# 1/sigma of a layer norm on all 128 partitions at once, in place of a column form that is spread by transposes

## The chip, the cores and the metric

The kernel runs on one core of one Trainium2 chip. The metric is the device time of one launch in microseconds (us). TensorE (PE) multiplies matrices; its weight loads are listed apart, as PEld. VectorE (DVE), ScalarE (ACT) and GpSimd (POOL) work on elements; SyncE (SP), POOL and ACT issue DMAs. An "execution" below is one profiled launch.

## What is computed

Four batches of 768 rows and 512 features go through a chunked attention, a mixer block and a second block. The change lies in the mixer block:

```python
u = x + mixed                                    # mixed: real part of a 2D FFT of x
mu = np.mean(u, axis=-1, keepdims=True)
var = np.mean((u - mu) ** 2, axis=-1, keepdims=True)
un = (u - mu) / np.sqrt(var + 1e-06)
ch = np.maximum(un @ w_ch1, 0.0) @ w_ch2
return (u + ch)
```

Since 1/sigma is one positive number for each row, the kernel multiplies the centred `u - mu` by both weight matrices first and scales the result by 1/sigma at the end.

## The kernel before, in words

Features lie on the partitions and rows of the batch in the free dimension. A *chunk* is 384 rows of one batch (`TC`), so there are eight; its centred input is `us`, four tiles of 128 features. Every matrix product is made of three float32r products of high and low parts (`split3`), accumulated in PSUM; line 65 issues nearly all of them.

Three stages follow each other. First the attention, the Fourier products and a first quarter of the mixer's hidden units (f = 0 to 3), in an order written out by hand (`SCHED`). Then the mixer's other hidden units, f = 4 to 15, in a loop over *steps* `s` and hidden tiles `f`; this is where the change is. Last the second block (`b1`, `conv`, `gate`, `b2`).

In the middle stage each turn of the loop runs `g1(s, f)` (12 products into a PSUM tile `h`; ACT takes the high part `hh`, DVE the low part `hl`), then a piece of the statistics, then `g2` of an earlier f (12 products into four `acc` tiles; two turns late, or one at the ends of a step). Chunks 0 to 4 are done in two steps (five hidden tiles, then seven); chunks 5 to 7 in one step of twelve. So the statistics generator `prep_stat(s)` runs eight times, one part for each turn `j` of the step: squares on ACT at j = 0, two adds on DVE at j = 1, nothing at j = 2, the sum over features at j = 3 (`pvar`), 1/sigma at j = 4, and at j = 5 the spreading (`prow`). `finish(s)` adds the `acc` tiles to `yp` and multiplies by the spread row `rb` (`d["r"]`).

Between these parts DVE and ACT decode weights for the next stage (`late()`, tiles `wsc`, `wlb`, `whb`, `wo`), paced by `PACE`, and split the next step's input into `uh` and `ul` (`split_uc`, at the last turn but one). Each engine executes its instructions in program order. The PSUM pool of `h`, `pvar` and `prow` has three buffers.

In the last chunk the loop also loads the second block's first input: `x_load(0, hf)` for the two halves, through the tile tag `sq` of the statistics, which has one buffer; each generator has three parts (the DMA on SP's queue, then twice a high part on ACT and a low part on DVE).

Where tiles lie (bytes from the start of a partition, as the program places them): pool `a1p` (`uh`, `ul`, `hh`, `hl`, `rb`) begins at 31,968 and is followed by `uc1` (`us`, `yp`, `sq` of 6,144 bytes each, and `st`, which takes 128) at 71,904; `wrb`, with the weight tiles of f = 8 to 15, at 90,464; `wra`, with the weight tiles of f = 4 to 7, at 163,808, where the last stage has its weights `wit`; `rx` at 196,576. In the last stage `xh` and `xl` of even batches lie in `rx`, those of odd batches in pool `w3p`, from byte 98,720 on. Weight slices are multiples of 512 bytes apart, slices of `uh`, `hh` and `xh` multiples of 1,536.

Of the kernel before, what the change touches and what calls it, by code (L numbers as in the profile page):

```python
# [7 lines left out]
F32 = mybir.dt.float32  # L8
F32R = mybir.dt.float32r
AF = mybir.ActivationFunctionType  # L10
ALU = mybir.AluOpType
# [14 lines left out]
TC = 384  # L26
# [19 lines left out]
def fourier_mixer_kernel(ctx: ExitStack, tc: tile.TileContext, qk, vw, w1, w2, w_in, w_out, conv_w,  # L46
                         mask, ident, dtab, orow, stab, sgn, out):
    nc = tc.nc
    mm = nc.tensor.matmul
# [12 lines left out]
    def accumulate(o, seq, start=True, stop=True):  # L62
        n = len(seq)
        for i, (a, b) in enumerate(seq):
            mm(o, a, b, start=(start and i == 0), stop=(stop and i == n - 1))  # L65

    const = ctx.enter_context(tc.tile_pool(name="const", bufs=1))
    epsc = const.tile([128, 1], F32, name="epsc")
    nc.vector.memset(epsc, 1e-6)
    onesm = const.tile([128, 128], F32, name="onesm")  # L70
# [5 lines left out]
    ident_sb = const.tile([128, 128], F32, name="ident_sb")  # L76
    stg = ctx.enter_context(tc.tile_pool(name="stg", bufs=2))
    rx = ctx.enter_context(tc.tile_pool(name="rx", bufs=1, side="right"))
    a1p = tc.alloc_tile_pool(name="a1p", bufs=2)
    ps_g = tc.alloc_tile_pool(name="ps_g", bufs=PSG, space=PSUM)  # L80
# [86 lines left out]
    def run(gen, n=1):  # L167
        for _ in range(n):
            if next(gen, "end") == "end":
                return False  # L170
        return True

    def rxt(tag, name):
        return rx.tile([128, 512 * NI], F32R, tag=tag, name=name)[:, 0:4 * TC].rearrange("p (k t) -> p k t", k=4)
# [3 lines left out]
    for nm, dst in (("a", w1h), ("b", w1l), ("c", w2h), ("d", w2l)):  # L178
        t = rx.tile([128, 512 * NI], F32R, tag=f"rx{nm}", name=f"rx{nm}")
# [329 lines left out]
    def x_load(b, hf, pool, tag="us"):  # L509
        ss = slice(hf * TC, hf * TC + TC)  # L510
        t = pool.tile([128, 4, TC], F32, tag=tag, name="xs")
        nc.sync.dma_start(out=t, in_=ucd[b][:, :, ss])
        yield
        if b % 2:
            xh, xl = (w3p.tile([128, 4, TC], F32R, tag=f"{n}{hf}", name=n) for n in ("xh", "xl"))
        else:
            xh, xl = rxt(("rxb", "rxa")[hf], "xh"), rxt(("rxd", "rxc")[hf], "xl")
        for k in range(0, 4, 2):
            if k:
                yield  # L520
            nc.scalar.copy(xh[:, k:k + 2], t[:, k:k + 2])
            nc.vector.tensor_tensor(out=xl[:, k:k + 2], in0=t[:, k:k + 2], in1=xh[:, k:k + 2].bitcast(F32),
                                    op=ALU.subtract)
        xs[b, hf] = (xh, xl)
# [53 lines left out]
    with tc.manual_schedule():  # L578
# [43 lines left out]
        ps_g.release()  # L622
        ps_g = tc.alloc_tile_pool(name="ps_g2", bufs=3, space=PSUM, reuse_waits="tile")
        uc1 = tc.alloc_tile_pool(name="uc1", bufs=1, reuse_waits="tile")
        NC1 = NB * S // TC
        NTC = TC // 128

        FS = (range(NI, NI + NGA), range(NI + NGA, NF1), range(NI, NF1))
        steps = [(c, FS[p], p == 1) for p in range(2) for c in range(NG2)] + [(c, FS[2], True) for c in range(NG2, NC1)]
        ck = {}  # L630

        def half(c):
            b, hf = divmod(c, 2)
            return b, slice(hf * TC, hf * TC + TC)

        def prep_load(s):
            b, ss = half(steps[s][0])
            us = (uc1.tile([128, 4, TC], F32, tag="us", name="us") if s % 3 == 0
                  else rxt(("rxa", "rxc")[s % 3 - 1], "us").bitcast(F32))
            nc.sync.dma_start(out=us, in_=ucd[b][:, :, ss])  # L640
            ck[s] = {"us": us}
# [7 lines left out]
        def late():  # L649
            stage = rx.tile([128, 512 * NI], F32, tag="rxd", name="wo")  # L650

            def place2(f):
                o = f[1] % 2 * 1024
                return stage[:, o:o + 512], stage[:, o + 512:o + 1024]

            yield from decode_all([(w_in[f], place2, ("i", f), wihd[f]) for f in range(NF2)]
                                  + [(w_out[f], place2, ("o", f), wohd[f]) for f in range(NF2)])
# [7 lines left out]
        def prep_stat(s):  # L665

            d = ck[s]
            c = steps[s][0]
            b, ss = half(c)
            sq = uc1.tile([128, 4, TC], F32, tag="sq", name="sq")  # L670
            for j in (0, 2):
                nc.scalar.activation(out=sq[:, j:j + 2], in_=d["us"][:, j:j + 2], func=AF.Square)
            nc.gpsimd.dma_start(out=ucd[b][:, :, ss], accum_op=ALU.add,
                                in_=mud[b][:, ss].rearrange("o (k t) -> o k t", k=1).to_broadcast([128, 4, TC]))
            yield
            nc.vector.tensor_tensor(out=sq[:, 0:2], in0=sq[:, 0:2], in1=sq[:, 2:4], op=ALU.add)
            nc.vector.tensor_tensor(out=sq[:, 0], in0=sq[:, 0], in1=sq[:, 1], op=ALU.add)
            yield
            yield
            p = ps_g.tile([128, 512], F32, tag="g", name="pvar")  # L680
            for t in range(NTC):
                mm(p[:, t:t + 1], sq[:, 0, t * 128:t * 128 + 128], onesm[:, 0:1], start=True, stop=True)
            st = uc1.tile([128, 4, NTC], F32, tag="st", name="st", bufs=2)
            ve, sd, r, e = (st[:, i] for i in range(4))
            nc.vector.tensor_scalar(out=ve, in0=p[:, 0:NTC], scalar1=0.5, scalar2=1e-6, op0=ALU.mult, op1=ALU.add)
            nc.scalar.activation(out=sd, in_=p[:, 0:NTC], func=AF.Sqrt, bias=epsc[:, 0:1], scale=0.5)
            yield
            nc.vector.reciprocal(out=r, in_=sd)
            nc.vector.tensor_tensor(out=e, in0=r, in1=r, op=ALU.mult)
            nc.vector.tensor_tensor(out=e, in0=e, in1=ve, op=ALU.mult)  # L690
            nc.vector.tensor_scalar(out=e, in0=e, scalar1=-0.5, scalar2=1.5, op0=ALU.mult, op1=ALU.add)
            nc.vector.tensor_tensor(out=r, in0=r, in1=e, op=ALU.mult)
            yield
            p = ps_g.tile([128, 512], F32, tag="g", name="prow")
            for t in range(NTC):
                nc.tensor.transpose(p[:, t * 128:t * 128 + 128], r[:, t:t + 1].to_broadcast([128, 128]), ident_sb)
            d["r"] = a1p.tile([128, TC], F32, tag="y", name="rb")
            nc.scalar.copy(d["r"], p[:, 0:TC])

        def g2(s, f):  # L700
            d = ck[s]
# [39 lines left out]
        stat, xg = iter(()), []  # L741
        for i, (s, f) in enumerate(seq):
            c, fs, last = steps[s]
            j, K = f - fs[0], len(fs)
            pace += [r for a, r in PACE if i >= a][-1]
            while pace >= 1.0:
                pace -= 1.0
                if not run(todo["W"]) and dec is None:
                    dec = todo["W"] = late()
            g1(c, f)  # L750
            if j == JL and s + 1 < len(steps):
                prep_load(s + 1)
            if j == 0 and last:
                stat = prep_stat(s)
            run(stat)
            if j == 2:
                prep_y(s)
            if j == K - JS and s + 1 < len(steps):
                for _ in split_uc(steps[s + 1][0], ck[s + 1]["us"]):
                    pass  # L760
            if s + 1 == len(steps):
                if j == 4:
                    for _ in todo["W"]:
                        pass
                    xg = [x_load(0, hf, uc1, "sq") for hf in range(2)]
                if 4 <= j < 10:
                    run(xg[(j - 4) // 3])
                if j == 7:
                    for n in range(NF2):
                        kind, fw = order[n]  # L770
                        wit.append(wra.tile([128, 1024], F32R, tag=f"w{kind}_{fw}", name=f"wit{n}"))
                        nc.gpsimd.dma_start(out=wit[n], in_=wihd[n])
            upto = i - 1 if i in ends or i - 1 in ends else i - 2
            while done <= upto:
                g2(*seq[done])
                done += 1
# [84 lines left out]
    with tc.manual_schedule():  # L861
        for h in hrow:
# [8 lines left out]
                                       op0=ALU.bitwise_and, op1=ALU.bitwise_or)  # L871
        nc.vector.tensor_scalar(out=cwi[1], in0=cwd[:, :, 1], scalar1=0xFFFFF, scalar2=0x100000,
                                op0=ALU.bitwise_and, op1=ALU.bitwise_or)
# [4 lines left out]
                                       op0=ALU.mult, op1=ALU.mult)  # L878
# [4 lines left out]
        for i in range(len(steps) + LAG):  # L883
# [12 lines left out]
            if i < len(steps):  # L896
                conv(b, f)
                if f == 0 and b + 1 < NB:
                    xg = [x_load(b + 1, hf, xsp) for hf in range(2)]
# [123 lines left out]
```

## Time and profile before

| what | value |
| --- | --- |
| median of 3 runs | 1041.53 us (1041.39 to 1042.96) |
| the profiled execution's own time | 1035.2 us |
| its span, first to last instruction | 1033.4 us |
| PE busy | 1019.8 us, 99% of the span |
| DVE, ACT, POOL busy | 638.1, 448.6, 187.7 us |
| granted TensorE clock | 0.998 of full speed |

The span is what the views of the trace divide; the profiled execution took 1.8 us more than its span, and 6.3 us less than the median of the runs. A matmul's listed duration overlaps the next one's, so the pace of a row of products is read from the distance of their starts, or from the chain of waits, which gives each piece of the path its own length.

### The profile page before, as it was taken

How to read it: one execution, taken by the hardware profiler on the slowest of the kernel's cores; microseconds unless marked ns; L12 is line 12 of the kernel's file. 1: busy time of each engine (PE TensorE's matmuls, PEld its weight loads, DVE VectorE, ACT ScalarE, POOL GpSimd, SP SyncE). 2: the span in 40 equal slices, each digit the busy share in tenths (PEclk: the TensorE clock that was granted, in tenths of full speed). 3: DMA queues.
4: the chain of work that ended last, by engine and by line, in shares of the span. 5: the costliest groups of instructions: out<-in, count | busy, mean ns of one | idle time of the engine just before them, and what ended most of it. 6: DMA issues, size and time to landing. Idle time of an engine off the chain costs nothing.

```text
span 1033.4 us, 16896 instructions
## 1 busy us (share of the span) xinstructions
PE 1019.8 (99%) x6548; PEld 972.6 (94%) x6548; DVE 638.1 (62%) x1489; ACT 448.6 (43%) x939; POOL 187.7 (18%) x215
## 2 busy tenths in 40 slices
PE   9999999999999999999999999999999999999998
PEld 7988989999999999999999999999989999999997
DVE  6788956757788765765565553513348656565554
ACT  6875665654434433333223232312236454454442
POOL 1442341422300000100000000001013222222222
PEclk9999999999999999999999999999999999999999
DMA  7854432521336555586989775353553211010101
GB/s 264 263 163 127 137 115 58 177 72 70 127 99 228 179 164 189 178 170 147 192 176 225 153 204 110 91 103 90 165 134 113 72 62 62 1 62 1 62 1 61
DMA packets 63776, 130.87 MB, mean 127 GB/s; under 512 B 4887, under 2 KB 39167, under 8 KB 63471
## 3 DMA queue, kind: packets, MB, share of 16 engines
q1 hardware_dynamic: 51424, 102.35, 29.9%
q0 software_dynamic: 12016, 27.16, 14.7%
q8 instruction: 51, 0.84, 0.3%
q10 hardware_dynamic: 256, 0.28, 0.1%
q14 instruction: 29, 0.24, 0.1%
HBM read 92.28 MB, written 43.79 MB: 132 GB/s over the span
## 4 chain that ended last, share of the span: by engine, by line
PE 92%; DVE 4%; DMA 2%; ACT 1%; issue 1%; POOL 0%; DVEq 0%; POOLq 0%; ACTq 0%
PE acc L65 32%; PE h L65 25%; PE ph L65 12%; PE y L65 7%; PE o L266 3%; PE z L65 3%; PE p L65 3%; PE sc L232 3%; PE atp L255 2%; PE idle L206 1%; DVE sm L238 1%; PE xtp L291 1%; DMA wot<-wohd 1%; DVE ul L165 1%; PE pm L415 1%
## 5 line engine op out<-in xcount | busy, mean ns | idle before, releaser
L65 PE MATMUL acc<-hh,w 128*128 128x384 f32 x768 | 211.2, 338 | 0.0
L65 PE MATMUL h<-uh,w 128*128 128x384 f32 x768 | 209.8, 337 | 0.0
L486 DVE SCALAR_TENSOR_TENSOR hl<-h,hh 128x384 fp32r<-128x384 f32 x128 | 70.5, 555 | 201.5 <-ACT hh L485 201.2
L485 ACT ACTIVATE hh<-h 128x384 fp32r<-128x384 f32 x128 | 62.4, 490 | 278.9 <-PE h L65 278.8
L65 PEld LDWEIGHTS acc<-hh,w 128*128 128x128 f32 x768 | 140.5, 188 | 0.0
L65 PEld LDWEIGHTS h<-uh,w 128*128 128x128 f32 x768 | 140.4, 188 | 0.0
L65 PE MATMUL ph<-xh,wit 128*128 128x384 f32 x512 | 136.3, 337 | 2.2 <-ACT hrow L813 2.2
L65 PE MATMUL acc<-hl,w 128*128 128x384 f32 x384 | 129.4, 337 | 0.1
L65 PE MATMUL h<-ul,w 128*128 128x384 f32 x384 | 129.2, 337 | 0.0
L65 PE MATMUL acc<-wot,hgh 128*128 128x512 f32 x384 | 119.7, 393 | 0.0
L821 DVE SCALAR_TENSOR_TENSOR cv<-hrow,cw_sb,cv 128x768 f32<-128x768 f32 x64 | 111.8, 1747 | 3.1 <-ACT cv L815 2.0
L65 PEld LDWEIGHTS ph<-xh,wit 128*128 128x128 f32 x512 | 93.3, 188 | 4.0 <-ACT hrow L813 2.8
L833 POOL TENSOR_TENSOR hgl<-cv,hgh 128x768 fp32r<-128x768 f32 x32 | 59.8, 1868 | 196.6 <-ACT hgh L832 174.5
L827 DVE TENSOR_TENSOR cv<-hrow,cv 128x768 f32<-128x768 f32 x32 | 30.7, 959 | 98.9 <-ACT cv L826 98.9
L65 PE MATMUL ph<-xl,wit 128*128 128x384 f32 x256 | 86.1, 336 | 0.0
L65 PEld LDWEIGHTS acc<-wot,hgh 128*128 128x128 f32 x384 | 71.7, 188 | 13.4
L246 ACT ACTIVATE sm<-sm,ngm 96x128 f32<-96x128 f32 x256 | 80.2, 393 | 5.8 <-DVE ngm L238 5.8
L813 ACT ACTIVATE hrow<-ph 128x384 f32<-128x384 f32 x64 | 31.2, 493 | 102.3 <-PE ph L65 101.1
L65 PE MATMUL acc<-wot,hgl 128*128 128x512 f32 x192 | 74.7, 389 | 0.0
L65 PEld LDWEIGHTS acc<-hl,w 128*128 128x128 f32 x384 | 72.2, 188 | 0.4 <-DVE hl L486 0.4
L65 PEld LDWEIGHTS h<-ul,w 128*128 128x128 f32 x384 | 72.1, 188 | 0.0
L238 DVE CUSTOM_DVE_ANT_0 sm<-sc,mask_sb 96x128 f32<-96x128 f32 x256 | 56.4, 282 | 15.7 <-PE sc L232 13.9
(145 smaller groups left out, 1836.8 us busy)
## 6 DMA issues: line engine op xcount, KB each, us to landing
w<-in_w SPq DMA_DIRECT2D x32, 512.0 KB, 3.9
qk<-in_qk SPq DMA_DIRECT2D x32, 448.0 KB, 4.0
us<-ucd SPq DMA_DIRECT2D x13, 768.0 KB, 5.3
yp<-yd SPq DMA_DIRECT2D x13, 768.0 KB, 9.1
vw<-in_vw SPq DMA_DIRECT2D x32, 260.0 KB, 3.1
ucd<-uc SPq DMA_DIRECT2D x8, 768.0 KB, 4.3
yd<-y SPq DMA_DIRECT2D x32, 192.0 KB, 2.4
ucd<-mud POOLq DMA_DIRECT2D x8, 768.0 KB, 17.3
```

The lines of the kernel that those rows point to most:

```text
L65: mm(o, a, b, start=(start and i == 0), stop=(stop and i == n - 1))
L232: mm(sch[2 * a + g], qT[64 * g:64 * g + 64, a, :], kT[64 * g:64 * g + 64, a, :], start=True, stop=True)
L238: nc.vector.tensor_tensor_reduce(out=sm[:, h, :], in0=sch[h], in1=mask_sb[:, kind, :], op0=ALU.add, op1=ALU.min, scale=-0.125, scalar=3e38 ...
L246: nc.scalar.activation(out=d["ex"][:, h, :], in_=d["ex"][:, h, :], func=AF.Exp, scale=-1.0, bias=d["ngm"][:, h:h + 1])
L255: nc.tensor.transpose(at[:, i, :], d["ex"][:, 4 * half + i, :], ident_sb[:QB, :QB])
L266: mm(oh[:, h // 4, h % 4, :], at_sb[:, h, :], vw[:, h * (HD + 1):(h + 1) * (HD + 1)], start=True, stop=True)
L485: nc.scalar.activation(out=hh, in_=p[:, 0:TC], func=AF.Relu)
L486: nc.vector.scalar_tensor_tensor(out=hl, in0=p[:, 0:TC], scalar=0.0, in1=hh.bitcast(F32), op0=ALU.max, op1=ALU.subtract)
L813: nc.scalar.activation(out=h[:, 1 + hf * TC:1 + hf * TC + TC], in_=p[:, 0:TC], func=AF.Relu)
L821: nc.vector.scalar_tensor_tensor(out=cv, in0=h[:, j:j + S], scalar=cw_sb[:, j, f:f + 1], in1=cv, op0=ALU.mult, op1=ALU.add)
L827: nc.vector.tensor_tensor(out=cv, in0=h[:, 1:S + 1], in1=cv, op=ALU.mult)
L833: nc.gpsimd.tensor_tensor(out=hgl[i], in0=cv, in1=hgh[i].bitcast(F32), op=ALU.subtract)
```

## The change

The sum over features becomes two float32r products with the 128 x 128 matrix of equal weights as stationary operand. Their result has the variance of all 384 rows on every partition, so 1/sigma is computed there on 128 x 384 elements in place of 128 x 3, and nothing is spread afterwards. The squares are split into a float32r part and a rest for it. The intermediate values reuse planes of `sq`; so the loads that go through `sq` in the last chunk move from j = 4 to j = 6.

```diff
         uc1 = tc.alloc_tile_pool(name="uc1", bufs=1, reuse_waits="tile")
+        onesr = uc1.tile([128, 128], F32R, name="onesr")
+        nc.vector.tensor_copy(onesr, onesm)
         NC1 = NB * S // TC
-        NTC = TC // 128
...
             nc.vector.tensor_tensor(out=sq[:, 0], in0=sq[:, 0], in1=sq[:, 1], op=ALU.add)
+            sqr = uc1.tile([128, 2, TC], F32R, tag="sqr", name="sqr")
+            nc.scalar.copy(sqr[:, 0], sq[:, 0])
+            nc.vector.tensor_tensor(out=sqr[:, 1], in0=sq[:, 0], in1=sqr[:, 0].bitcast(F32), op=ALU.subtract)
             yield
             yield
             p = ps_g.tile([128, 512], F32, tag="g", name="pvar")
-            for t in range(NTC):
-                mm(p[:, t:t + 1], sq[:, 0, t * 128:t * 128 + 128], onesm[:, 0:1], start=True, stop=True)
-            st = uc1.tile([128, 4, NTC], F32, tag="st", name="st", bufs=2)
-            ve, sd, r, e = (st[:, i] for i in range(4))
-            nc.vector.tensor_scalar(out=ve, in0=p[:, 0:NTC], scalar1=0.5, scalar2=1e-6, op0=ALU.mult, op1=ALU.add)
-            nc.scalar.activation(out=sd, in_=p[:, 0:NTC], func=AF.Sqrt, bias=epsc[:, 0:1], scale=0.5)
-            yield
-            nc.vector.reciprocal(out=r, in_=sd)
+            accumulate(p[:, 0:TC], [(onesr, sqr[:, i]) for i in range(2)])
+            ve, e = sq[:, 2], sq[:, 3]
+            r = d["r"] = a1p.tile([128, TC], F32, tag="y", name="rb")
+            nc.vector.tensor_scalar(out=ve, in0=p[:, 0:TC], scalar1=0.5, scalar2=1e-6, op0=ALU.mult, op1=ALU.add)
+            nc.scalar.activation(out=sq[:, 1], in_=p[:, 0:TC], func=AF.Sqrt, bias=epsc[:, 0:1], scale=0.5)
+            yield
+            nc.vector.reciprocal(out=r, in_=sq[:, 1])
+            yield
             nc.vector.tensor_tensor(out=e, in0=r, in1=r, op=ALU.mult)
             nc.vector.tensor_tensor(out=e, in0=e, in1=ve, op=ALU.mult)
             nc.vector.tensor_scalar(out=e, in0=e, scalar1=-0.5, scalar2=1.5, op0=ALU.mult, op1=ALU.add)
             nc.vector.tensor_tensor(out=r, in0=r, in1=e, op=ALU.mult)
-            yield
-            p = ps_g.tile([128, 512], F32, tag="g", name="prow")
-            for t in range(NTC):
-                nc.tensor.transpose(p[:, t * 128:t * 128 + 128], r[:, t:t + 1].to_broadcast([128, 128]), ident_sb)
-            d["r"] = a1p.tile([128, TC], F32, tag="y", name="rb")
-            nc.scalar.copy(d["r"], p[:, 0:TC])
...
+                if j == 6:
                     xg = [x_load(0, hf, uc1, "sq") for hf in range(2)]
-                if 4 <= j < 10:
-                    run(xg[(j - 4) // 3])
+                if 6 <= j < 12:
+                    run(xg[(j - 6) // 3])
```

In `uc1` the change adds `onesr` (512 bytes) and `sqr` (3,072) and drops `st`; `wrb`, which follows, then begins at byte 93,920 in place of 90,464. `a1p`, `wra`, `rx` and `w3p` stay where they are.

## Rows read from the trace of the kernel before

**Rows 1.** The page, part 1: busy time, share of the span, instructions.

```profile
PE 1019.8 (99%) x6548; PEld 972.6 (94%) x6548; DVE 638.1 (62%) x1489; ACT 448.6 (43%) x939; POOL 187.7 (18%) x215
```

**Rows 2.** Busy time by stretch: the middle stage with the statistics.

```profile
440.00:758.00 318.00, 318.00 (x1839) 317.68 (x1838) 152.97 (x302) 87.87 (x159) 22.05 (x23) 1.00 0.64 148
```

**Rows 3.** Chain of waits, 440 to 770 us: start, length, what; first and last statistics.

```profile
463.07 0.56 PE pvar L682 x6
463.63 2.22 PE acc L65 x12
...
472.18 0.33 PE prow L696 x3
472.51 2.11 PE acc L65 x12
...
480.96 2.11 PE h L65 x12
...
718.70 0.56 PE pvar L682 x6
...
727.76 0.33 PE prow L696 x3
```

**Rows 4.** Chain of waits, 345 to 445 us: f = 4 to 8.

```profile
379.44 2.08 PE acc L65 x12
381.53 2.11 PE h L65 x12
...
387.80 2.08 PE h L65 x12
389.88 2.11 PE acc L65 x12
```

**Rows 5.** Chain of waits, last stage: an even batch, then an odd one.

```profile
808.18 4.19 PE ph L65 x24
...
816.49 4.24 PE ph L65 x24
```

**Rows 6.** Groups by line and form: shapes, count, busy us, mean ns.

```profile
L677 DVE TENSOR_TENSOR sq<-sq 128x384 f32<-128x384 f32 x8 | 4.5, 558 | 0.3
L294 DVE TENSOR_SCALAR xT<-xtp 128x384 f32<-128x384 f32 x1 | 0.5, 544 | 0.0
L123 DVE TENSOR_SCALAR wsc<-w 128x512 int32<-128x512 int32 x48 | 21.7, 452 | 3.0 <-DMA w<-in_w 1.4
L688 DVE RECIPROCAL st<-st 128x3 f32<-128x3 f32 x8 | 1.3, 167 | 0.0
L269 DVE RECIPROCAL r<-r 96x8 f32<-96x8 f32 x32 | 6.4, 199 | 1.1
L698 ACT COPY rb<-prow 128x384 f32<-128x384 f32 x8 | 3.8, 474 | 0.0
```

**Rows 7.** Chain of waits, 160 to 180 us: a plain float32 product of 384 columns.

```profile
166.92 0.67 PE pm L415 x2
```

**Rows 8.** Timeline of DVE, turns 1 and 4 to 6 of the first statistics.

```profile
458.81 0.56 DVE L677 TENSOR_TENSOR sq<-sq 128x384 f32<-128x384 f32 x1
...
468.59 0.56 DVE L486 SCALAR_TENSOR_TENSOR hl<-h,hh 128x384 fp32r<-128x384 f32 x1 [2.41 <-ACT hh L485]
...
473.90 1.83 DVE L165 TENSOR_TENSOR ul<-us,uh 128x768 fp32r<-128x768 f32 x2 [0.54 <-ACT uh L162]
...
477.35 0.56 DVE L486 SCALAR_TENSOR_TENSOR hl<-h,hh 128x384 fp32r<-128x384 f32 x1 [1.02 <-ACT hh L485]
```

**Rows 9.** Timeline of the last chunk: SP's load, DVE's turn 5, ACT's last turn.

```profile
719.35 15.81 SPq L512 DMA_DIRECT2D xs<-ucd  x2
...
728.38 0.56 DVE L486 SCALAR_TENSOR_TENSOR hl<-h,hh 128x384 fp32r<-128x384 f32 x1 [2.75 <-ACT hh L485]
...
753.47 0.49 ACT L485 ACTIVATE hh<-h 128x384 fp32r<-128x384 f32 x1 [3.73 <-PE h L65]
```

**Rows 10.** Instructions by tile, `xs`: time from issue to landing.

```profile
DMA to landing us min/median/max: 6.7/7.9/9.1
```

## Prediction

> **What bounds the kernel now.** I read the page's busy times first, then the chain of waits through the stage that holds the change, then the busy times of that stretch, then single groups and timelines for prices. The page shows PE busy for 99% of the span, the next engine for 62% [rows 1]. In the stretch from 440 to 758 us PE is busy all 318.00 us and DVE 152.97 of them, 48% [rows 2]. The chain of waits runs through PE alone there: products in groups of 12, and for each of the eight chunks one piece of `pvar` and one of `prow` between them [rows 3]. So in this stage an instruction costs what it lengthens PE's row, and work on DVE or ACT costs nothing until PE waits for it. The first group behind `pvar` is listed with 2.22 us where others have 2.11 [rows 3]; those 0.11 us belong to `pvar`.
>
> The same view has a second thing to see. Groups of 12 products do not all take the same time: 2.08 us with the weights of f = 4 to 7, 2.11 with those of f = 8, both for `h` and for `acc`, side by side in one step [rows 4]. In the last stage 24 `ph` products take 4.19 us in an even batch and 4.24 in an odd one [rows 5]. The work is the same; what differs is the pool in which an operand lies: weights in `wra` against `wrb`, `xh` in `rx` against `w3p`. The places of front explain it in one way: all fast operands begin 224 bytes past a multiple of 256 (31,968, 163,808, 196,576), the weights in `wrb` 96 bytes past one (90,464), `xh` in `w3p` 160 (98,720). They allow another: slow operands lie in the middle of the partition, between 90,464 and 163,808, fast ones outside.
>
> **The change part by part.** *PE, removed.* `pvar` costs 0.56 + 0.11 = 0.67 us, `prow` 0.33 [rows 3]: 1.00 us for a chunk, 8.0 for eight.
>
> *PE, added.* Two products of 128x128 by 128x384 float32r, the form of `h` and `acc`: 2.11 / 12 = 0.176 us each [rows 3], 0.35 for a chunk, 2.8 for eight. Net gain 8.0 - 2.8 = 5.2 us. A bound from the other side is the plain float32 product of 384 columns, 0.67 us [rows 7]: two of these, 1.34, would cost 8 x 0.34 = 2.7 us more than what goes. I take the float32r price, since both operands are declared so.
>
> *Placement.* `wrb` moves from 90,464 to 93,920, which is 224 past a multiple of 256, like every fast operand. It holds the weights of eight of the twelve hidden tiles: 5 x 24 products in the first steps, 5 x 7 x 24 in the second, 3 x 8 x 24 in the long ones, 1,536 in all or 128 groups of 12. If they fall to the fast pace, 128 x (2.11 - 2.08) [rows 4] = 3.8 us are gained on top; if place in the partition is what counts, nothing, as `wrb` stays in the middle. I take the 3.8, because the second reading needs the range of slow places to end within some 11,700 bytes between the last weights of `wrb` (151,904) and the first of `wra`, while the first covers rows of two stages, weights and moving data, with one rule. Both ends stay in the range.
>
> [...]
>
> *DVE.* Gone for a chunk are seven tiny operations less the one that stays, about 6 x 0.16 = 1.0 us with the reciprocal's 0.167 [rows 6]. New at 384 columns: four TENSOR_TENSOR of 0.558 (one subtract, three in the correction), a TENSOR_SCALAR from PSUM of 0.544, one from SBUF of about 0.452 x 384 / 512 = 0.34 [rows 6], and the reciprocal. The trace has this only at 3 columns (0.167) and 8 (0.199), 6.4 ns for a column [rows 6]: 0.167 + 381 x 0.0064 = 2.6 us. Below, it is bounded by the 0.558 of a TENSOR_TENSOR; I take 2.6, as the slope comes from the operation itself. Together 2.23 + 0.54 + 0.34 + 2.6 - 1.0 = 4.7 us for a chunk, 38 for eight: DVE's 153 of 318 us become 191, 60%. ACT gets a copy, a longer root, and loses the copy of `rb`: under 0.5 us a chunk.
>
> What hides it, in the times of the first chunk [rows 8, 3]: `hl` of turn 4 ends at 469.15, the reciprocal at 471.8, a piece of decoding (0.7) at 472.5, and `hl` of turn 5 comes at 472.8 as before. Behind it the four correction operations (2.0), `ul` of the next step (1.83) and a piece of decoding end at 478.0, and `hl` of turn 6 moves from 477.35 to 478.0. PE needs `ul` at 480.96 and that `hl` after it. With ACT's decoding copies that queue behind DVE's, I count 3 us of cover. So the price is zero up to a reciprocal of some 5.6 us.
>
> *The wait added.* PE now waits for the subtract at turn 1. The second add ends at 459.4 [rows 8], ACT's copy (0.47) and the subtract (0.56) at 460.5; PE comes to `pvar` at 463.07 [rows 3]. Behind it on PE stand all products, but there are 2.6 us to spare. `h` tiles fare better: `prow` no longer takes one of three PSUM buffers.
>
> *The moved loads.* Before, SP started the first load at 719.35, once `pvar` had read `sq` [rows 9]. Now it must wait until the correction has read `sq` at turn 5, 728.9 + 2.0 = 731, and lands by 738.9 at the median, 740.1 at worst [rows 10]; conversions follow at turns 7 and 8. The second load starts near 743 and lands by 752.1 at worst; its conversions at turns 10 and 11 queue behind the last `hh` at 753.47 [rows 9], whose 24 last products give 4 us more. SP has nothing urgent behind these loads. Price zero; were a landing 4 us later, about 3 us once.
>
> *Onesr.* One DVE copy, under 0.2 us, once, beside PE's work.
>
> **Sum.** 5.2 + 3.8 = 9.0 us less on PE's row. The profiled execution would go from 1035.2 to 1026.2, its span from 1033.4 to 1024.4; the runs, whose median lies 6.3 us above the profiled execution, from 1041.5 to 1032.5.
>
> **The rivals.** *A, the forecast*: both gains, 1032.5. *B, the products in `wrb` keep 2.11*: only the 5.2 us, 1036.3. [...] *C, `wrb` at some third pace*, since 224 past a multiple of 256 is seen for weights only at 480 past a multiple of 512, and 93,920 is 224 past: anything from 1030 to 1041. *D, slower: the reciprocal.* If it takes over 5.6 us, `ul` of the next step is late and PE stands at the first `h` of each following step; from 6.7 us (17 ns a column, 2.7 times the slope of the rows) it eats the whole gain, at 8 us it costs 8 x 2.4 = 19 us, 1051.7. *E, no gain: the sum runs as plain float32* and the pace in `wrb` stays: 1041.5 + 2.7 = 1044.2.
>
> **How the numbers follow.** Chances: A 0.50, B 0.33, C 0.08, D 0.05, E 0.04. The likeliest is 1032.5. The range reaches from a little under A to a little over B, since the two hold most of the chance: 1030.5 to 1037.5; the one or two us beyond them are for the scatter of the runs (1041.39 to 1042.96). Faster by over 0.2% (2.1 us, about what a measurement of this kernel can tell from no change): A, B and most of C and a little of D, 0.92; within it: 0.04; slower: 0.04.
>
> **What would show it.** In the profile after: PE still at 99%; in the chain two products of `pvar` in about 0.35 us a chunk, no `prow`; groups of f = 8 and above at 2.08 (A) or 2.11 (B); RECIPROCAL 128x384 near 2.6 us; no wait of PE for `ul`, `hl` or `pvar`'s operands; the first `ph` as soon after the last `acc` as before. The forecast is wrong if the chain in this stage leaves PE, or if those groups stay at 2.11.

## The result, and the profile after

The median of four runs goes from 1041.47 us (1041.39 to 1042.96) to 1031.78 us (1027.97 to 1032.75); the ratio is 0.9903, with a 95% interval of 0.9885 to 0.9921. The forecast was 1032.5, with a range of 1030.5 to 1037.5.

The page's first part after the change, to be read beside [rows 1]:

```profile
PE 1015.4 (99%) x6492; PEld 968.1 (94%) x6492; DVE 674.1 (65%) x1498; ACT 452.8 (44%) x939; POOL 187.9 (18%) x215
```

PE still fills the span. DVE grew by 674.1 - 638.1 = 36.0 us, and PE did not wait for it but for one gap of 0.2 us. Busy time in the middle stage, up to the end of its last product (columns as in [rows 2]):

```profile
440.00:753.70 313.70, 313.70 (x1810) 313.46 (x1809) 192.23 (x318) 93.46 (x163) 23.45 (x25) 1.00 0.68 158
```

DVE is at 192.23 of 313.70 us, 61%, where it had 48%. The chain of waits, 440 to 770 us, which answers to [rows 3] (start, length, what):

```profile
467.33 0.35 PE pvar L65 x2
467.68 2.08 PE acc L65 x12
...
526.26 0.54 PE pvar L65 x2
...
715.41 0.35 PE pvar L65 x2
...
749.03 4.69 PE acc L65 x27
753.75 2.12 DVE yp L718 x4
```

Three things are to be seen. `prow` is gone. `pvar` takes 0.35 us where 0.56 + 0.11 stood, except once, 0.54 in the third chunk. And the groups of 12 show 2.08, where this view had 2.11. The same view over 345 to 445 us, with the first `acc` group of f = 4 and then the first `h` and `acc` groups of f = 8, which [rows 4] had at 2.11:

```profile
359.05 2.20 PE acc L65 x11
...
386.21 2.08 PE h L65 x12
...
394.53 2.08 PE acc L65 x12
```

I measure the middle stage from the second product on `acc` with f = 4 (359.05; 354.32 before) to the first addition to `yp` of the last chunk (753.75; 758.22 before). The second product, since in most executions it waits for `hl` and the row of products is closed only from there. The same two pieces in the kernel before:

```profile
354.32 2.18 PE acc L65 x11
...
758.22 2.14 DVE yp L720 x4
```

The stage went from 403.90 to 394.70 us: 9.2 us less, where the sum said 9.0.

The profiled executions alone would mislead. Their spans are 1033.4 and 1029.4, only 4.0 apart, although 9.2 went in the middle stage. Nearly all of the rest is ahead of the change, in a stage with the same code: the middle stage begins 4.73 us later (what lies behind it took 0.5 us more). Busy time from 100 to 110 us, before and then after (behind the five engines' busy times stand the clock granted to PE, as a share of full speed, the DMA share and GB/s):

```profile
100.00:110.00 10.00, 9.82 (x83) 8.74 (x84) 8.00 (x20) 6.37 (x19) 3.54 (x5) 0.83 0.23 77
```

```profile
100.00:110.00 10.00, 9.57 (x52) 8.59 (x54) 6.25 (x15) 4.43 (x13) 2.87 (x5) 0.56 0.14 53
```

PE got 0.83 of its clock in one execution and 0.56 in the other, each a mixture of two levels, 1.00 and 0.50, and issued 83 and 52 products in the same 10 us. In both, PE had just stood idle for 2.20 us, waiting for POOL's `gs`. After that the trace has PE's granted clock at 0.50 for 3.4 us before the change; with it for 10.2 us, and for 3.4 more from 135 us on, after three short waits for `hl` (0.43, 0.28 and 0.45 us). At 0.50 the float32r products of 384 columns in the second of these stretches start 0.32 us apart; at 1.00, in the fast groups of the middle stage, 0.173. By this the 10.2 us more at the lower level cost an estimated 10.2 x (1 - 0.173 / 0.32) = 4.7 us, which is the 4.73. The total varies from execution to execution: further runs of the kernel before gave 1033.68 to 1043.47 us. In the middle stage the granted clock was 1.00 in both. So from here on kernels are compared over the middle stage.

### The profile page after: what moved, and what is told of

It is laid out like the page before. It is cut to its first block, busy times and chain, and to the rows that moved or that the text cites. A ratio compares the mean times of both kernels' runs of the same rounds, so it can differ in the third digit from the quotient of the medians.

```text
span 1029.4 us, 16779 instructions
## 1 busy us (share of the span) xinstructions
PE 1015.4 (99%) x6492; PEld 968.1 (94%) x6492; DVE 674.1 (65%) x1498; ACT 452.8 (44%) x939; POOL 187.9 (18%) x215
## 4 chain that ended last, share of the span: by engine, by line
PE 93%; DVE 4%; ACT 1%; DMA 1%; issue 0%; POOL 0%; DVEq 0%; POOLq 0%; ACTq 0%
PE acc L65 32%; PE h L65 25%; PE ph L65 12%; PE y L65 7%; PE o L266 3%; PE sc L232 3%; PE p L65 3%; PE z L65 3%; PE atp L255 2%; PE idle L206 1%; DVE sm L238 1%; PE xtp L291 1%; DVE ul L165 1%; PE pm L415 0%; DMA qk<-in_qk 0%
## 5 line engine op out<-in xcount | busy, mean ns | idle before, releaser
L65 PE MATMUL acc<-hh,w 128*128 128x384 f32 x768 | 208.0, 334 | 0.0
```

## The experiments

**The theory** is that of the forecast: two gains that have nothing to do with each other, 5.2 us from the statistics' products and 3.8 us from the place of the weights in `wrb`, with DVE's work hidden. The rivals: the pace was set by something else that the change brought (neighbours in time, DVE's load), or by the region of the partition; DVE's cover is nearly used up; and the split in two parts is not worth its two operations.

**One: the change with `wrb` moved back to 96 past a multiple of 256.** An unused tile ahead of it moves its start to 94,048.

```diff
         onesr = uc1.tile([128, 128], F32R, name="onesr")
         nc.vector.tensor_copy(onesr, onesm)
+        uc1.tile([128, 32], F32, name="pad")
```

> The changed kernel with an unused tile of 128 bytes in uc1, so that the weights in wrb begin at byte 94,048, again 96 past a multiple of 256; the statistics stay as changed. Place theory (a product's pace depends on where its operands start within 256 bytes): groups of 12 products with f = 8 to 15 go back from 2.08 to 2.11 us, the middle stage is 3.8 us longer, the time about 1035.6 us. Rival (the middle of the partition is slow or fast for another reason, or the pace has to do with the statistics): groups stay at 2.08, the time at 1031.8.

Measured: 1034.65 us median (1030.19 to 1037.19, 10 runs), ratio to the kernel before 0.9943 (0.9921 to 0.9965). The middle stage takes 398.73 us, 4.03 more than with the change as it is. Chain of waits, the two ends of the stage (352.84, 751.57) and the first groups of f = 8:

```profile
352.84 2.20 PE acc L65 x11
...
359.20 2.11 PE h L65 x12
...
367.56 2.11 PE acc L65 x12
...
751.57 2.14 DVE yp L719 x4
```

The groups of f = 8 are slow again, with the same instructions, the same DVE load and the weights 128 bytes further on.

**Two: the kernel before, with `wrb` at 224.** The same tile, in the kernel before; `wrb` starts at 90,592.

```diff
         uc1 = tc.alloc_tile_pool(name="uc1", bufs=1, reuse_waits="tile")
+        uc1.tile([128, 32], F32, name="pad")
```

> The kernel before with the same unused tile of 128 bytes in uc1, so that wrb begins at byte 90,592, which is 224 past a multiple of 256; the statistics stay in column form. Place theory: groups with f = 8 to 15 fall from 2.11 to 2.08 us and the time by 3.8 us to about 1037.7, with nothing of the change's work. Rival: groups stay at 2.11, the time at 1041.5.

Measured: 1037.28 us median (1032.43 to 1039.82, 10 runs), ratio 0.9971 (0.9948 to 0.9993). The middle stage takes 399.94 us, 3.96 less than before. Chain of waits, the two ends of the stage (359.06, 759.00; the second product did not wait here), the first groups of f = 8 and the first statistics:

```profile
359.06 2.17 PE acc L65 x12
...
365.38 2.08 PE h L65 x12
...
373.70 2.08 PE acc L65 x12
...
467.30 0.56 PE pvar L683 x6
...
476.30 0.33 PE prow L697 x3
...
759.00 2.12 DVE yp L721 x4
```

The statistics are those of before, the groups of f = 8 those of the change. With the first experiment this fills a square of middle stages:

| | `wrb` at 96 | at 224 | difference |
|---|---|---|---|
| statistics of before | 403.90 | 399.94 | 3.96 |
| statistics of the change | 398.73 | 394.70 | 4.03 |
| difference | 5.17 | 5.24 | |

Within 0.1 us each gain is what it is whether or not the other is there, and they add to the 9.2. What lies next to these groups in time, and DVE's load, are out as causes of the pace: with the statistics and DVE's work of before the groups are fast here, and with those of the change they were slow in the first experiment. An unused tile of 128 bytes, which changes no computation, is 43% of what the change brought. The region of the partition is out: in these two kernels `wrb` moves by 128 bytes within it.

**Three: a ladder.** In the change, each weight tile of `wrb` is followed by 32 unused bytes, so that the tiles start 32 bytes further past a multiple of 256 each time. The moving operands (`uh`, `ul`, `hh`, `hl`) stay at 224.

```diff
+            wrb.tile([128, 8], F32, tag=f"pad{kind}_{f}", name="pad")
```

> The changed kernel with 32 unused bytes behind each of the 16 weight tiles of wrb, so that their starts climb from 224 (modulo 256) in steps of 32: the tiles that h reads (f = 8 to 15) start at 224, 32, 96, 160, 224, 32, 96, 160, those that acc reads at 0, 64, 128, 192, 0, 64, 128, 192; the moving operands start at 224 as before. Place theory in its narrow form: only h at f = 8 and 12 keeps 2.08 us, the others take 2.11 or so, and f = 8 to 11 repeat in f = 12 to 15. If the place counted modulo 512, f = 12 would differ from f = 8. Rival (region): 2.08 everywhere.

**Four: the same ladder, with the moving operands at 96.** A tile of 128 bytes among the constants moves every pool on the left by 128, `wrb` too; `wra` (f = 4 to 7) lies on the right and stays at 224.

```diff
+    const.tile([128, 32], F32, name="padc")
```

> The ladder of the run before with 128 unused bytes more in the pool of constants, so that all tiles on the left move by 128: uh, ul, hh and hl, the moving operands, start 96 past a multiple of 256, the weights of h in wrb at 96, 160, 224, 32 and again, those of acc at 128, 192, 0, 64 and again; weights in wra stay at 224. If each operand counts by itself, the moving operands alone make every group slow, 2.11 or more, f = 4 to 7 too. If the distance of weights and moving operand counts, h at f = 8 and 12 (96 against 96) is at 2.08 and f = 4 to 7 (224 against 96) at 2.11. If the weights alone count, h at f = 10 and 14 and all of f = 4 to 7 are at 2.08.

Measured: 1035.66 and 1036.40 us, one execution each. Chain of waits in the last long step, first the third kernel, then the fourth:

```profile
707.12 2.08 PE h L65 x12
...
711.32 4.16 PE h L65 x24
...
726.23 2.12 PE h L65 x12
...
734.63 2.08 PE h L65 x12
```

```profile
707.42 2.11 PE h L65 x12
...
711.65 4.22 PE h L65 x24
...
726.75 2.10 PE h L65 x12
...
730.95 2.11 PE h L65 x12
...
735.16 2.08 PE h L65 x12
```

The pieces at 707 and 711 are `h` of f = 4, 5 and 6, whose weights did not move at all: 2.08 and 4.16 became 2.11 and 4.22 when the moving operand went from 224 to 96. So in these groups it is not where the weights start that counts, but the two operands together. The pieces at 726 and 727 are `h` of f = 9, those at 735 of f = 11, and the one at 730.95 of f = 10. The mean time from one product's start to the next within a group, times 12, worked out from the starts in the two traces and the addresses in the two programs, by how far the weights start past the moving operand, modulo 256:

| distance, bytes | tile | third kernel, us | fourth kernel, us |
|---|---|---|---|
| 0 | `h` f = 8; 12 | 2.080; 2.105 | 2.093; 2.105 |
| 32 | `acc` f = 8; 12 | 2.086; 2.096 | 2.088; 2.095 |
| 64 | `h` f = 9; 13 | 2.121; 2.121 | 2.107; 2.118 |
| 96 | `acc` f = 9; 13 | 2.080; 2.080 | 2.080; 2.080 |
| 128 | `h` f = 10; 14 | 2.110; 2.110 | 2.111; 2.110 |
| 160 | `acc` f = 10; 14 | 2.122; 2.123 | 2.123; 2.123 |
| 192 | `h` f = 11; 15 | 2.077; 2.080 | 2.077; 2.080 |
| 224 | `acc` f = 11; 15 | 2.123; 2.123 | 2.117; 2.122 |

With both operands moved by 128 the two columns agree within 0.014 us. The kernel before had distance 128 (96 - 224), the change has 0. The place theory in its narrow form fails in the third kernel already: weights that start at 160 (`h` of f = 11 and 15) and at 64 (`acc` of f = 9 and 13) run at 2.08 too.

Distances 0 and 32 show values from 2.08 to 2.105, and f = 12 differs from f = 8, which the expectation had set as the sign of a count modulo 512. Single products say more: in the third kernel `h` of f = 12 takes 185, 176 and 182 ns from start to start for its first three products and 173 for each that follows, the pace of f = 8; at a distance of 160 the whole group goes 180, 175, 178, 174 ns, over and over (medians over eight groups). So at 0, in f = 12, only the head of the group is slow. A count modulo 512 does not explain it: f = 4 to 7 lie at the same distance modulo 512 as f = 12, and three of these four run at 2.08 from their first product on. What sets the head is open.

**Five: the last stage.** If distance decides, `xh` in `w3p` should be mended like the weights: it starts 160 past a multiple of 256 and its weights 224 past one, a distance of 64, which is slow in the table (2.107 to 2.121 us). An unused tile of 64 bytes puts it at 224.

```diff
+    w3p.tile([128, 16], F32, name="pad3")
```

> The changed kernel with 64 unused bytes behind cw_sb in w3p, so that xh and xl of odd batches and the high and low parts hgh and hgl of the last stage start at 224 modulo 256 in place of 160, at distance 0 from wit and wot. Distance theory: the 24 ph products of odd batches go from 4.24 to 4.19 us, 16 pieces or 0.8 us in all; the acc products of that stage (4.12 to 4.13 for 18) may also come nearer to what their 512 columns need, up to 1.3 us more, which no row shows yet. Time 1029.7 to 1031.0. Rival (what was seen belongs to the middle stage alone): no difference, 1031.8.

Measured: 1028.87 us median (1025.23 to 1031.60, 6 runs), ratio 0.9900 (0.9867 to 0.9933) to the kernel before, which had 1039.20 in these rounds. Chain of waits in the last stage at an odd batch, the change first, then this kernel:

```profile
811.98 4.24 PE ph L65 x24
816.21 4.13 PE acc L65 x18
...
1008.16 13.76 PE acc L65 x60
```

```profile
811.31 4.18 PE ph L65 x24
815.50 4.12 PE acc L65 x18
...
1006.55 13.66 PE acc L65 x60
```

All batches now run at the pace of the even ones [rows 5], so the rival is out. From the fifth hidden tile of the first batch to the last group (778.75 to 1008.16 and 778.09 to 1006.55) it takes 228.46 us where it took 229.41, so 0.95 us, and the last group 0.10 less. The 0.8 us of `ph` came; the up to 1.3 us that `acc` might bring were the author's estimate and no run shows them: some 0.2 came. The traces show that gain; the runs cannot tell 1028.87 from 1031.78, since their ranges overlap and the kernel before was 2 us faster in these rounds as well.

**Six and seven: the reciprocal two and three times.** The same operation again, so that DVE is late by 2.55 or 5.1 us more for each chunk.

```diff
             nc.vector.reciprocal(out=r, in_=sq[:, 1])
+            nc.vector.reciprocal(out=r, in_=sq[:, 1])
```

> The changed kernel with the reciprocal issued twice with the same operands, 5.1 us of DVE in place of 2.5 for each chunk. By the cover that the prediction counted (3 us beyond the 2.6), PE's row stays closed: the middle stage, from the first acc products at f = 4 to the last yp adds, keeps its 394.7 us within 0.5. Rival (DVE already is at its edge, as the 0.54 us for pvar in the third chunk may suggest): 8 x 2.5 = 20 us more.

> The changed kernel with the reciprocal three times, 7.6 us for each chunk, 2.0 beyond the 5.6 from which the prediction expected PE to wait. If the cover was counted rightly, PE waits for ul or hl in each following step, up to 8 x 2 = 16 us in all, less in the last three chunks, where decoding has ended or the step is long; so 5 to 16 us more. If the cover is larger than counted, nothing or little.

Measured: 1030.87 and 1035.71 us, one execution each. With two reciprocals the middle stage (358.88 to 753.56) is 394.68 us, the same as with one, though the second costs as much as the first (groups by form: count, busy, mean ns):

```profile
L692 DVE RECIPROCAL rb<-sq 128x384 f32<-128x384 f32 x8 | 20.4, 2552 | 0.3
L691 DVE RECIPROCAL rb<-sq 128x384 f32<-128x384 f32 x8 | 20.3, 2542 | 0.0
```

With three it is 397.83 (360.76 to 758.59), 3.1 more, and the chain leaves PE after the first statistics:

```profile
474.17 0.56 DVE hl L486
474.72 2.47 DVE rb L691
477.22 2.56 DVE rb L692
479.81 2.55 DVE rb L693
...
485.33 0.96 DVE ul L165
...
486.33 2.20 PE h L65 x11
```

PE stands at the first `h` of the next step and waits for `ul`, as rival D had it, but for less. From one `pvar` to the next it takes 29.89 us here (469.04 to 498.93) where the change takes 29.47 (467.33 to 496.80): 0.42 for a chunk. Four chunks lose that, the third 1.40, the last three, which lie in the long steps, nothing. I had expected 5 us at the least for the third reciprocal, so DVE's cover was larger than I counted: with 5.1 us more it lacked 0.42, so in the ordinary chunk it has 5.1 - 0.42 = 4.7 us to spare behind a reciprocal of 2.54, and in the third 3.7.

**Eight: one plain float32 product for the sum.** This leaves out the split into two parts, ACT's copy and DVE's subtract, and multiplies `sq` by `onesm`.

```diff
-            accumulate(p[:, 0:TC], [(onesr, sqr[:, i]) for i in range(2)])
+            mm(p[:, 0:TC], onesm, sq[:, 0], start=True, stop=True)
```

> The changed kernel with the sum over features as one plain float32 product of sq with onesm, without the split into two float32r parts (no cast on ACT, no subtract on DVE); the tile of the parts stays allocated, so all places stay. From the plain float32 product of the kernel before, 0.67 us: pvar takes 0.67 in place of 0.35 us in the chain, the middle stage 8 x 0.32 = 2.6 us more. Rival (a float32 product of 384 columns costs no more than two float32r ones): no difference.

Measured: 1032.63 us, one execution; middle stage 396.89 us (358.52 to 755.41), 2.19 more. Chain of waits at the first statistics:

```profile
466.81 0.64 PE pvar L683 x2
```

The float32 product takes about 0.65 where the two float32r ones take 0.35: 8 x 0.30 = 2.4, less the 0.2 that the third chunk no longer waits. So the split is worth 2.2 us, and the other 5.2 - 2.2 = 3.0 us of the statistics' gain come from dropping narrow products and transposes alone.

## Why the prediction was right

*PE's row sets the end*: right; the chain runs on PE through the whole stage, with one gap of 0.2 us.

*The statistics' products*, 8.0 gone and 2.8 added, net 5.2: the square shows 5.17 and 5.24. From the starts of single products, with all groups at the fast pace (experiment two against the change), `pvar` and `prow` cost 0.67 and 0.36 us a chunk, 8.3 in all, and the two new products 0.35, 3.0 in all with the one wait of 0.2: both terms were a little small, and what they lacked cancels. Both bounds were on the table, and the operand type decided: 0.35 us for two float32r products, 0.65 for one float32 product (experiment eight; [rows 7] had 0.67).

*Placement*, 3.8: the square shows 4.0, and the groups of f = 8 went from 2.11 to 2.08 with it and back without it. The outcome was right; the reason was too narrow. "All fast operands begin 224 bytes past a multiple of 256" held in the kernel before only because nearly everything else begins there too. In experiment four weights at 224 were slow (2.11 us), as the moving operand had left 224. In the two ladders the pace went with the distance between the two (2.08 us at 96 and 192, 2.11 to 2.12 at 128 and 160), and 224 was right for `wrb` because the moving operands lie at 224, a distance of 0 (2.08 us for `h` of f = 8 after the change). The rows of before could not tell the two rules apart, so that this term came true was in part luck. (The gap that the second reading had to fit into is 163,808 - 151,904 = 11,904 bytes, not 11,700; nothing hangs on it.) The second reading, the middle of the partition, is refuted: 128 bytes do it. Rival C, a third pace for `wrb`, did not come: 224 past a multiple of 512 was as good as 480 (2.08 us for `wrb` after the change, as for `wra`).

DVE's load did not change the pace as far as the runs go: with DVE busy for 61% of the stretch in place of 48%, the fast groups still take 2.08 us. PE's own two operands did: 12 products take 2.08 to 2.12 us by the distance between them. Whether it is the load of the weights that slows the product, no run here shows.

*DVE*, 38 us more, hidden: 36.0 more, hidden but for one gap of 0.2 us. The rows that answer to [rows 6], groups by form:

```profile
L691 DVE RECIPROCAL rb<-sq 128x384 f32<-128x384 f32 x8 | 20.4, 2544 | 0.0
L681 DVE TENSOR_TENSOR sqr<-sq,sqr 128x384 fp32r<-128x384 f32 x8 | 4.5, 559 | 4.7 <-ACT sqr L680 4.7
L688 DVE TENSOR_SCALAR sq<-pvar 128x384 f32<-128x384 f32 x8 | 4.4, 548 | 0.0
```

The reciprocal was forecast at 2.6 from two points at 3 and 8 columns, and takes 2.54 at 384; no row had vouched for a straight line that far. (On 3 columns the kernel before had six operations on DVE, not seven; the sum of about 1.0 us that the forecast took off is right.) What stands behind it, in the timeline of DVE after the first statistics, beside [rows 8]:

```profile
472.93 2.54 DVE L691 RECIPROCAL rb<-sq 128x384 f32<-128x384 f32 x1
475.39 0.63 DVE L128 SCALAR_TENSOR_TENSOR wlb<-w,wlb 128x512 int32<-128x512 int32 x1
476.62 0.56 DVE L486 SCALAR_TENSOR_TENSOR hl<-h,hh 128x384 fp32r<-128x384 f32 x1 [0.60 <-ACT hh L485]
...
479.14 1.82 DVE L165 TENSOR_TENSOR ul<-us,uh 128x768 fp32r<-128x768 f32 x2
```

Behind the reciprocal DVE still sat idle for 0.60 us until ACT's `hh`. *The cover* was the mis-sized term: 3 us by count, 4.7 by experiments six and seven. And rival D's price was too high: I charged every microsecond of lateness to all eight chunks, but the last three statistics lose none. "Zero up to 5.6 us" is about 2.54 + 4.7 = 7.2, and a reciprocal of 7.65 cost 3.1 us in all, not the whole gain.

*The wait added*, with 2.6 us to spare: in the first chunk the subtract ends at 464.87 and PE comes at 467.33, 2.5 us to spare. In the third chunk the subtract starts only at 525.74, behind the four additions and two products that finish a chunk (L718, L724) and four operations of decoding, and PE waits 0.2 us. The forecast looked at the first chunk alone. Price 0.2 us, once.

*The moved loads*, price zero. Landing, from the instructions by tile ([rows 10] had 7.9 at the median), and the last conversion in ACT's timeline ([rows 9] had the last `hh` at 753.47):

```profile
DMA to landing us min/median/max: 5.1/6.0/7.0
```

```profile
749.46 0.83 ACT L521 CAST xh<-xs 128x768 fp32r<-128x768 f32 x1
```

SP starts the first load at 727.36 (719.35 before), the conversions end at 750.29 behind the last `hh`, and PE does not wait for them.

*The step that failed* is the way from the sum to the profiled execution: 1026.2 with a span of 1024.4 was forecast, 1031.14 with 1029.4 came, because I held the rest of that execution fixed and the attention stage's clock was not. Against the median, the same sum fits: 1032.5 and 1031.78. That it fits so closely is in part luck, as the median of the kernel before itself lay at 1041.47, 1041.52 and 1039.20 us in the three sets of runs.

## What to carry to other kernels

When one operation's groups run at two paces with the same work, look at where both operands lie, and test it with an unused tile of a few dozen bytes before looking for a cause in time. Any edit that adds or drops a tile moves all that follows it in its pool (here 128 unused bytes alone were worth 3.96 us), so a change should be timed with the layout held, or its gain is partly the layout's. And the row of the engine that bounds the time can be read in single products, while what the other engines have to spare is worth testing by doing an operation of theirs twice: here a second reciprocal cost nothing and the third 3 us.

## What the runs showed of the hardware that was not expected

In the two ladders the pace of the 128x128 by 128x384 float32r products went with the distance between their weights' and their moving operand's start, taken modulo 256: 2.08 us for 12 at 96 and 192, 2.11 to 2.12 at 64, 128, 160 and 224, and values from 2.08 to 2.105 at 0 and 32. At 0, in `h` of f = 12 of the third kernel, the first three products were slow (185, 176 and 182 ns) and the others not (173). Between the two ladders, which differ by 128 in both operands, the times of 12 differ by 0.014 us at most. Why these distances, and what sets the pace at 0 and 32, stays open: no run changed the distance by less than 32 or exchanged neighbouring groups.
